# Two chained attentions on one core: weight loads in longer runs, a last block in halves, and a new hand-off table

## The chip, the cores and the metric

The kernel runs on one core of one Trainium2 chip. The metric is the device time of one execution in microseconds. The median of three runs of the kernel before is 152.31 us (150.82 to 152.47).

## What is computed

Two layers follow each other. The first is an attention with 8 heads of 64 over 768 positions, for a batch of 4, where a query sees the 8 first keys and the 96 last ones, with a bias that falls with the distance. The second is a mixture of 4 experts: each expert is a causal attention over the first layer's output, and each position adds the results of its two best experts, weighted by the gate.

```python
keep = is_global | is_local            # key < 8, or 0 <= row - key < 96
scores = np.where(keep, scale * q @ k.T - slope * dist, -1e9)
x = softmax(scores) @ v                # per head; heads side by side: B, S, 512
logits = x @ w_gate                    # the two largest of 4 -> weights w
for e in range(4):
    ye = softmax(causal(scale * (x @ wq[e]) @ (x @ wk[e]).T)) @ (x @ wv[e]) @ wo[e]
    out += (e is one of the two) * w * ye
```

## The kernel before

The rows of the batch make 24 units of 128 positions (`u`, 6 to a batch entry). Every step of a unit is a small function, a stage, and a table written as text, `ORDER` (line 791), lists the stages of all units in the order in which they are issued: two letters, the unit, and the engine of its copy (a ScalarE, g GpSimd, v VectorE) or the queue of its load (s SyncE, a ScalarE). The loop at line 765 walks through it. Each engine runs its own instructions in this order, so the table decides what is queued behind what. It comes from a planner outside the file.

The stages that matter here, in the order of a unit:

- `lk`, `lq`, `lv` (`load`, line 235): 256 KB of k, q or v as 1,024 runs of 256 bytes into one of six buffers for each of the three. `kc`, `qc` (line 256) cast to fp16; `vc`, `vx` (line 260) cast v into a ring.
- `tk`, `tq` (line 270): TensorE transposes; `tq` ends with a copy to SBUF. `gi`, `gs`: scores against the global keys. `sa`, `sb` (line 332): local scores in PSUM, with the bias added by a matmul (line 345), then an exponential on ScalarE (line 355).
- `vg`, `va`, `vb` (lines 363 and 374): the products with v. They go into a PSUM tile of which there is one buffer (`psZ`), eight heads side by side, 65 columns each, the 65th for the row sum. `vb` ends with a reciprocal (388) and a product (390) on VectorE, which leave x in fp16.
- `tx` (line 396) transposes x; `pk`, `pq` (line 405) and `pv` (line 423) project it with the weights; `ro` takes one step of the choice of experts.
- `ca`, `cb`, `cc` (line 442): causal scores and exponentials (462); `ma`: GpSimd sets the part above the diagonal to zero (474); `za`, `zb` (line 477): products with v for four experts, in the same single PSUM buffer, then reciprocal, weight and product on VectorE (494, 496, 498).
- `tz` (line 501) transposes the result, `ou` (line 514) multiplies it with wo, copies it out of PSUM (522) and stores it. Both take PSUM buffers from `psT`, which has two; scores use two of `psS`.
- `wi` and `wc` (lines 153 and 169) load and cast the weights: 0 is wk, 1 wq, 2 wv, 3 wo, 4 the gate. For 0 to 2 row d of a weight goes to partition d mod 128, so that each run of the load has 256 bytes.
- `wm` (`keep_warm`, line 241): so many matmuls of the identity, 240 columns each, into columns that nobody reads.
- `ck` (line 734) checks that all row sums lie in a safe range. At the end their count is loaded into registers (line 780), and a branch (782) goes to a general path if some did not. `bh` places a hint for this branch.

SyncE issues 56 of the 72 loads, two of the weight loads (wo and the gate) and all 24 stores; ScalarE issues 16 loads and three weight loads between its activations.

Of the kernel before, what the change touches and what calls it, by code (L numbers as in the profile page):

```python
# [18 lines left out]
P = 128  # L19
# [3 lines left out]
def kernel(  # L23
# [28 lines left out]
    NH = 3  # L52
# [30 lines left out]

    def bias_constants(_):
        V.tensor_copy(rel[:, :], rel_i[:, :])
        ge = const.tile([P, W], F32, name="ge")
        V.tensor_scalar(ge[:, :], rel[:, :], 0.0, None, op0=Alu.is_ge)
        lt = const.tile([P, W], F32, name="lt")
        V.scalar_tensor_tensor(lt[:, :], rel[:, :], float(NL), ge[:, :],
                               op0=Alu.is_lt, op1=Alu.mult)  # L90
        V.tensor_scalar(lt[:, :], lt[:, :], -1.0, -NEG, op0=Alu.add, op1=Alu.mult)
        V.tensor_scalar(rel[KB:P, :], rel[KB:P, :], slopes[1] / slopes[0], None, op0=Alu.mult)
        for p in range(NP):
            V.scalar_tensor_tensor(biasT[:, p, :], rel[:, :], -slopes[2 * p] / sc1, lt[:, :],
                                   op0=Alu.mult, op1=Alu.add)
# [57 lines left out]
    def weights_in(i, on):  # L153

        issue = queues[on]
        if i == 4:
            w32s[i] = wst.tile([P, NK, E], F32, name="wg32", tag="wg32", bufs=1)
            issue(w32s[i][:, :, :], moe_w_gate.rearrange("(ko kp) e -> kp ko e", kp=P))
            return
        w32s[i] = wst.tile([P, E, NK, Hd], F32, name="w32", tag="w32")  # L160
        if i < 3:
            issue(w32s[i][:, :, :, :],
                  (moe_wk, moe_wq, moe_wv)[i].rearrange("e (ko kp) d -> kp e ko d", kp=P))
# [35 lines left out]
    NC, current = 120, {}  # L199
# [33 lines left out]
    s16s, zs_, x16s, routing, zss, zts, tps, ppss, zs2 = ({} for _ in range(9))  # L233
# [7 lines left out]
    def keep_warm(n):  # L241
# [5 lines left out]
        for _ in range(n):  # L247
            mm(current["z"][:, 0, 4 * P - 2 * NC:4 * P].rearrange("r (a n) -> r a n", a=2),  # L248
               lhsT=ident[:, :], rhs=ident[:, 0:NC].unsqueeze(1).to_broadcast([P, 2, NC]),
               start=alone, stop=True, skip_group_check=True)  # L250
            alone = False
# [108 lines left out]
    def global_values(u):  # L360
# [3 lines left out]
        for hf in range(2):  # L364
            r = slice(hf * Dh, hf * Dh + Dh)
            mm(zs_[u][:, hf, 0:HG * VW].rearrange("r (h d) -> r h d", h=HG),  # L366
# [3 lines left out]
    def local_values(u, i):  # L370
# [4 lines left out]
        for hq in (2 * i, 2 * i + 1):  # L375
            for prev in range(2 if ri else 1):
                for c in range(2):
                    for hf in range(2):
                        r = slice(hf * KB, hf * KB + KB)
                        at = c * (2 * P - KB) + prev * P  # L380
                        mm(zs_[u][:, hf, hq * VW:(hq + 1) * VW],  # L381
# [3 lines left out]
        if i == 1:  # L385
            z4 = zs_[u][:, :, 0:HG * VW].rearrange("r a (h d) -> r a h d", h=HG)
            rinv = rinv1[:, b, ri, :].rearrange("r (a h) -> r a h", a=2)
            V.reciprocal(rinv, z4[:, :, :, Dh])
            x16s[u] = pp.tile([P, 2, HG, Dh], F16, name="x16", bufs=5)
            V.tensor_tensor(x16s[u][:, :, :, :], z4[:, :, :, 0:Dh],  # L390
                            rinv.unsqueeze(3).to_broadcast([P, 2, HG, Dh]), op=Alu.mult)

    def turn_x(u, on):

        xTs[u] = pp.tile([P, NK, P], F16, name="xT", bufs=4)
        x16 = x16s[u][:, :, :, :].rearrange("r a h d -> r (a h d)")
# [80 lines left out]
    def causal_values(u, i):  # L477
# [6 lines left out]
        z_ps = zs2[u][:, 0, 0:E * VW].rearrange("r (e d) -> r e d", e=E)  # L484
        for e in range(i * E // 2, (i + 1) * E // 2):
            for ci in range(n):
                mm(z_ps[:, e, :], lhsT=a2[:, e % 2, (e // 2) * n + ci, :],  # L487
                   rhs=held("v2buf", b * NT + ci)[:, e, :], start=(e == 0 and ci == 0), stop=True,
                   skip_group_check=True)
        if i == 0:  # L490
            return
        assert next(routing[u // NH], "end") == "end"
        rinv = rinv2[:, b, ri, :]
        V.reciprocal(rinv, z_ps[:, :, Hd])
        ce = pp.tile([P, E], F32, name="ce")
        V.tensor_mul(ce[:, :], rinv, wts[u // NH][:, ri % NH, :])
        zss[u] = pp.tile([P, E, Hd], F16, name="zs")
        V.tensor_tensor(zss[u][:, :, :], z_ps[:, :, 0:Hd],  # L498
                        ce[:, :].unsqueeze(2).to_broadcast([P, E, Hd]), op=Alu.mult)

    def turn_z(u, on):
        zts[u] = pp.tile([P, NEP, P], F16, name="zt")
        if on == "s":
            nc.sync.dma_start_transpose(zts[u][:, :, :],
                                        zss[u][:, :, :].rearrange("r e d -> r (e d)"))
            return
        zt_ps = psT.tile([P, NEP, P], F16, name="ztps", tag="t")
# [6 lines left out]
    def output(u, on):  # L514
        b, ri = divmod(u, NT)
        assert 3 in ready
        o_ps = psT.tile([P, D], F32, name="ops", tag="t")
# [5 lines left out]
        dma(out[b, ri * P:(ri + 1) * P, :], o_sb[:, :])  # L523

# [34 lines left out]
    def general_path(ctx):  # L559
# [35 lines left out]

        ident32 = gc.tile([P, P], F32, name="ident32")
# [20 lines left out]
        with tc.For_i(0, B, 1) as b:  # L617
# [43 lines left out]
            for ri in range(NT):  # L661
                l_ps = gp.tile([P, MAXB], F32, name="gs", tag="s", bufs=2)
                for ko in range(NK):
                    mm(l_ps[:, 0:E], lhsT=xT[:, ko, ri * P:(ri + 1) * P],
                       rhs=wvg16[:, ko, E * Hd:E * Hd + E],
# [6 lines left out]
            for e in range(E):  # L672
                for w, dst, nm in ((wq16, qs, "q"), (wk16, ks, "k")):
                    d = gb.tile([Hd, S], F16, name=f"g{nm}T{e}")
                    for c in range(2):
                        p_ps = gp.tile([P, MAXB], F32, name="gs", tag="s", bufs=2)
                        for ko in range(NK):
                            mm(p_ps[0:Hd, 0:S // 2], lhsT=w[:, ko, e // 2, e % 2, :],
# [6 lines left out]
                for ct in range(NT):  # L685
                    p_ps = gp.tile([P, MAXB], F32, name="gs", tag="s", bufs=2)
                    for ko in range(NK):
                        mm(p_ps[:, 0:Hd], lhsT=xT[:, ko, ct * P:(ct + 1) * P],
                           rhs=wvg16[:, ko, e * Hd:(e + 1) * Hd],
# [55 lines left out]
    def branch_hint(_):  # L745

        tc.mark_branch_hint_location("general", hint="LikelyTaken", engines=(
            mybir.EngineType.PE, mybir.EngineType.Activation, mybir.EngineType.DVE))
# [5 lines left out]
        "vs": (select_values,), "xb": (bias_constants,), "xi": (half_identities,),  # L754
# [9 lines left out]
    }  # L764
    for slot in ORDER.split():
        stage, *args = stages[slot[:2]]
        if slot[-1].isalpha():
# [7 lines left out]
    n_f = const.tile([1, 1], F32)  # L775
    V.reduce_sum(n_f[:, :], n_ps[:, :], axis=Ax.X)
    n_i = const.tile([1, 1], I32)
    V.tensor_copy(n_i[:, :], n_f[:, :])
# [13 lines left out]
xb0 lk0s kc0v lq0s az0v az1g lk1s xi0a xs0v xk0g lq1a wm14 tk0 qc0g lv0s kc1g lk2s lq2s lk3a  # L792
wm5 tq0a lq3s xc0g lv1a lv2s lq4s lk4a qc1v lq5s vc0g vx0g wm4 tk1 tq1v xm0v lk5s wm10 sa0 sb0
wm10 vs0 gi0 wi0a wm2 gs0 lk6s kc2v qc2v tk2 tq2v wm3 gs1 lq6s wm7 vg0 kc3g va0 vb0 vc1g vx1v
qc3a sa1 az2g sb1 tk3 tq3v tx0v wi1a vg1 az3g qc4a vc2g kc4g vx2v wm2 va1 wm4 sa2 sb2 vb1 qc5g
gs2 kc5a wc0g tk4 tq4v tx1v az4v lv3s vg2 va2 lv4s vb2 sa3 sb3 tk5 tq5v wm6 tx2v kc6a lq7s wi2a
qc6v wm4 sa4 sa5 tk6 vc3g tq6v pk0 sb4 sb5 wc1v pk1 wm2 gs3 wm2 pq0a vx3v pq1a gi1 vg3 vc4g
vx4g wi4s lv5s va3 vb3 lk7a ca0 ma0 pk2 pq2v tx3v ca1 vg4 va4 vb4 lq8s ca2 pk3 pq3a lk8s vc5v
vx5v cb2 vg5 wc2g lv6s kc7g lq9s pv0v pv1v lq10a lk9s qc7g qc8g kc8g ca3 cb3 tk7 lv7s tq7v pv2v
ro0 va5 sa6 tk8 tq8v tx4v vc6g vx6g lk10a lk11s vb5 sb6 gs4 lv8s ro0 pv3v pk4 qc9g pq4v ro0 ro0  # L800
lq11s lq12a ma1 vs1 lk12s lk13a sa7 tx5v kc9g pv4v kc10g ma2 vg6 va6 ro0 vb6 ca4 tk9 tq9v pk5
lk14s lq13s lv9a pq5v cb4 tx6v sb7 vc7v qc10g qc11a vx7g vc8g tk10 tq10v pv5v kc11g kc12g lq14a
qc12g cc4 vg7 va7 lq15s vb7 ro0 ro0 pk6 pq6a tk11 tq11v vx8g sa8 sb8 tx7v lk15s kc13g kc14g za0
qc13g zb0 lv10a tk12 tq12v gi2 pv6a sa9 sa10 ro1 ro1 lv11s lv12s vc9v vg8 va8 vb8 pk7 pq7a vx9g
tk13 tq13v lk16s lk17s gs5 ca5 qc14g lq16s tz0v za1 lq17s ro1 tk14 tq14v zb1 tx8a ro1 sb9 vc10g
vx10g sb10 kc15a pv7v pv8v vc11g vg9 va9 kc16a vb9 sa11 sa12 tz1v ro1 lq18s kc17v pk8 pq8a za2
ro1 tk15 zb2 sb11 sb12 qc15g tq15v tx9a vc12g vx11g vg10 va10 lk18s vx12g qc16g qc17v vb10 gs6
vs2 tk16 tq16v wi3s qc18g kc18g tk17 tq17v ma3 cb5 vg11 ma4 lk19s va11 lv13s lv14s cc5 tx10v
lv15s tk18 tq18v vb11 ca6 pv9v pv10a ro1 sa13 ro2 sa14 lq19s lq20s gi3 lq21s wc3g za3 ro2 zb3
ou0v ou1a vc13g ro2 ca7 lq22s ca8 vx13g vg12 ma5 va12 vb12 tx11v pk9 pq9v za4 ro2 lk20s kc19g  # L810
zb4 lk21s lk22s lv16s ma6 tz2a ro2 sb13 sa15 tx12v qc19v qc20g pk10 pq10a vc14g vx14g kc20g ma7
tz3v vg13 vc15g ro2 va13 vb13 lv17a cb8 gs7 ma8 ou2v tk19 tq19v lk23s lv18a za5 sb14 sb15 tz4v
zb5 tx13a pv11v sa16 ro2 sb16 vg14 va14 vb14 pk11 ro3 lv19s lv20a pq11a pv12v sa17 za6 zb6 ro3
ro3 vc16g vx15g vx16g ou3a ou4v qc21v ca9 lv21s cb9 tk20 kc21g tq20v za7 pk12 zb7 pq12a tx14v
vc17g ca10 vx17g ro3 cb10 vg15 va15 qc22g tz5v tz6v vb15 ou5a vc18g vc19g tk21 tq21v sa18 vc20v
sb17 kc22g kc23g za8 zb8 tx15a pk13 pq13v ca11 vg16 cc10 va16 pv13v lv22a pv14v cb11 ma9 vb16
gs8 ou6a pk14 pq14v ca12 vx18g vg17 va17 vb17 ca13 tz7v ro3 pk15 ro3 ro3 vx19v pq15a sb18 vs3
tx16v tx17v za9 zb9 ro4 pk16 lq23s pq16a ou7v ro4 lv23s qc23g cc11 vg18 va18 vc21g vb18 pv15a
tk22 tq22v sa19 sa20 ma10 pv16v ma11 za10 tz8a zb10 sb19 sb20 ro4 ro4 ro4 pv17v tz9v ca14 vg19
va19 vb19 ou8a ou9a vx20v sa21 sb21 ro4 ro4 tk23 tq23v ro5 za11 tx18v zb11 tz10a sa22 sb22  # L820
tx19v ma12 pv18v cb14 vg20 va20 vb20 gs9 ro5 ou10a pv19v ma13 vx21g ca15 ca16 vc22g za12 tz11v
zb12 pk17 pq17v pk18 pq18v ro5 ma14 ro5 vc23g cb15 vx22g vg21 va21 vb21 cb16 ro5 tx20v ro5 ro5
pk19 pq19a za13 zb13 pv20a ro6 sa23 sb23 tx21v vg22 va22 vb22 cc16 tz12v pk20 ro6 pq20a za14
# [47 lines left out]
```

## Time and profile before

| | before |
|---|---|
| median of 3 runs | 152.31 us (150.82 to 152.47) |
| profiled execution: its time, its span | 152.97 us, 150.8 us |
| TensorE busy | 140.3 us, 3,029 matmuls |
| VectorE, ScalarE, GpSimd busy | 111.4, 108.1, 90.2 us |
| DMA | 85,364 packets, 27.77 MB, 82,000 of them under 512 bytes |
| filler matmuls (line 248) | 75 |

The span runs from the first to the last instruction; the time of an execution holds some 2 us more around it. TensorE is PE in the views, its weight loads PEld, VectorE DVE, ScalarE ACT, GpSimd POOL, SyncE SP; a q after the name is the engine's instruction queue. A group of instructions is named by its line, its engine and the tiles that it writes and reads, and an entry of the chain by its start and its length in microseconds.

### The profile page before, as it was taken

Reading aid. Unit: us, or ns where it says so; the run is one execution under the profiler, and the core shown is the slowest. Engines: PE = TensorE matmul, PEld = TensorE weight load, DVE = VectorE, ACT = ScalarE, POOL = GpSimd, SP = SyncE. Lnnn points to the kernel's source line nnn. Section 1 sums busy time; section 2 is a strip of 40 time slices with the busy share of each in tenths; the row PEclk is TensorE's granted clock in tenths of the full one; section 3 lists DMA queues with packets and bytes.
Section 4 is the critical chain, followed back from the end, with each engine's and each line's share of the span. In section 5 each row is a group of like instructions: output and inputs, shape, how many; then the busy total and the mean of one; then the engine's idle time right before and its main releaser. Section 6 shows DMA issues by size and latency. Waiting matters only on the chain.

```text
span 150.8 us, 7217 instructions
## 1 busy us (share of the span) xinstructions
PE 140.3 (93%) x3029; PEld 110.2 (73%) x3029; DVE 111.4 (74%) x348; ACT 108.1 (72%) x176; POOL 90.2 (60%) x254
## 2 busy tenths in 40 slices
PE   5799999999999999999978999999999999999760
PEld 4567778887778888878757778888778878786520
DVE  4838676687899887878863987687787777778850
ACT  4027657778576888888638998887977978989640
POOL 7278351568878988797827899136286345463200
PEclk9999999999999999999999999999999999999999
DMA  4999998999999989899899963415221005013462
GB/s 99 280 252 286 276 261 192 254 247 238 277 282 275 245 201 249 189 256 208 231 240 288 301 166 113 116 43 142 74 77 70 4 19 195 24 51 127 155 263 97
DMA packets 85364, 27.77 MB, mean 184 GB/s; under 512 B 82000, under 2 KB 82000, under 8 KB 85328
## 3 DMA queue, kind: packets, MB, share of 16 engines
q1 hardware_dynamic: 62496, 21.51, 56.6%
q10 hardware_dynamic: 22832, 5.77, 17.1%
q8 instruction: 24, 0.39, 1.0%
q14 instruction: 12, 0.10, 0.2%
HBM read 20.98 MB, written 6.29 MB: 181 GB/s over the span
## 4 chain that ended last, share of the span: by engine, by line
PE 74%; DMA 11%; DVE 4%; POOL 3%; ACT 2%; issue 1%; SPq 1%; ACTq 0%; POOLq 0%; DVEq 0%
PE pps L414 14%; PE cps L459 7%; PE vps L428 7%; PE tp L283 7%; PE ops L519 6%; PE zps L487 6%; PE zps L381 6%; PE sps L345 5%; PE zps L248 4%; DMA kf<-in_k_dram 4%; DMA vf<-in_v_dram 4%; PE xps L402 3%; PE sps L352 3%; DMA qf<-in_q_dram 3%; PE zps L366 2%; PE ztps L509 2%
## 5 line engine op out<-in xcount | busy, mean ns | idle before, releaser
L462 ACT ACTIVATE a<-cps 128x1024 f16<-128x1024 f32 (+1 forms) x48 | 42.2, 917 | 8.3 <-PE cps L459 6.6
L355 ACT ACTIVATE abuf<-sps 128x636 f16<-128x636 f32 (+1 forms) x48 | 30.6, 686 | 12.8 <-PE sps L352 10.1
L267 POOL CAST vbuf<-vf 64x256 f16<-64x256 f32 x76 | 31.0, 408 | 8.4 <-DMA vf<-in_v_dram 5.2
L474 POOL TENSOR_SCALAR_AFFINE_SELECT a<-a 128x256 f16<-128x256 f16 x48 | 18.3, 409 | 5.1 <-ACT a L462 4.8
L285 DVE COPY kqT<-tp 128x1024 f16<-128x1024 f16 x23 | 15.7, 688 | 6.6 <-PE tp L283 6.1
L390 DVE TENSOR_TENSOR x<-zps,rinv 128x512 f16<-128x512 f32 x24 | 16.6, 691 | 0.8
L487 PE MATMUL zps<-v2buf,a 128*128 128x65 f16 x336 | 16.0, 193 | 0.6 <-DVE zs L498 0.5
L345 PE MATMUL sps<-biasT,ident 64*64 64x318 f16 (+1 forms) x192 | 14.5, 305 | 1.4 <-ACT abuf L355 1.3
L381 PE MATMUL zps<-vbuf,abuf 64*128 64x65 f16 x704 | 15.5, 189 | 0.0
L258 POOL CAST s16k<-kf 128x512 f16<-128x512 f32 x17 | 10.3, 612 | 8.7 <-DMA kf<-in_k_dram 8.3
L487 PEld LDWEIGHTS <-a 128*128 128x128 f16 x336 | 13.3, 97 | 2.1 <-DVE zs L498 0.9
L381 PEld LDWEIGHTS <-abuf 64*128 64x128 f16 x704 | 14.0, 94 | 1.1 <-issue 0.2
L414 PE MATMUL pps<-xT,wk 128*128 128x128 f16 x192 | 14.7, 219 | 0.0
L414 PE MATMUL pps<-xT,wq 128*128 128x128 f16 x192 | 14.5, 219 | 0.0
L248 PE MATMUL zps<-ident 128*128 128x240 f16 x75 | 12.8, 316 | 1.7 <-POOL ident masks.py:199 1.6
L428 PE MATMUL vps<-wvg,xT 128*128 128x260 f16 x96 | 13.9, 275 | 0.0
L459 PEld LDWEIGHTS <-kq 64*128 64x128 f16 x336 | 9.7, 94 | 5.8 <-issue 4.4
L459 PE MATMUL cps<-kq,kq 64*128 64x128 f16 x240 | 13.8, 218 | 0.0
L519 PE MATMUL ops<-wo,zt 128*128 128x512 f16 x48 | 13.5, 380 | 0.4 <-DVE zt L512 0.4
L352 PE MATMUL sps<-kqT 64*64 64x159 f16 (+2 forms) x384 | 13.8, 223 | 0.0
L258 POOL CAST s16q<-qf 128x512 f16<-128x512 f32 x15 | 9.4, 630 | 5.1 <-DMA qf<-in_q_dram 4.9
L414 PEld LDWEIGHTS <-wk 128*128 128x128 f16 x192 | 11.5, 98 | 0.8
(113 smaller groups left out, 286.4 us busy)
## 6 DMA issues: line engine op xcount, KB each, us to landing
out_dram<-osb SPq DMA_DIRECT2D x24, 256.0 KB, 2.3
qf<-in_q_dram SPq DMA_DIRECT2D x20, 256.0 KB, 5.6
kf<-in_k_dram SPq DMA_DIRECT2D x19, 256.0 KB, 5.7
vf<-in_v_dram SPq DMA_DIRECT2D x17, 256.0 KB, 5.5
vf<-in_v_dram ACTq DMA_DIRECT2D x7, 256.0 KB, 4.7
kf<-in_k_dram ACTq DMA_DIRECT2D x5, 256.0 KB, 4.9
qf<-in_q_dram ACTq DMA_DIRECT2D x4, 256.0 KB, 4.5
w<-in_moe_wk_dram ACTq DMA_DIRECT2D x1, 512.0 KB, 5.3
```

The lines of the kernel that those rows point to most:

```text
L248: mm(current["z"][:, 0, 4 * P - 2 * NC:4 * P].rearrange("r (a n) -> r a n", a=2), lhsT=ident[:, :], rhs=ident[:, 0:NC].unsqueeze(1).to_bro ...
L258: copies[on](s16s[nm, u][:, :, :], fs[nm, u][:, :, :])
L267: copies[on](o[hf * KB:(hf + 1) * KB, c, :, 0:Dh], fs["v", u][c * KB:(c + 1) * KB, hf * HG:(hf + 1) * HG, :])
L345: mm(s_ps[o, hh, 0:2 * w].rearrange("r (c n) -> r c n", c=2), lhsT=ident2[r, :], rhs=biasT[r, p, 0:w].unsqueeze(1).to_broadcast([KB, 2, w] ...
L355: S_.activation(as_[u][:, :, g, :].rearrange("r h (c n) -> r h c n", c=2)[:, :, :, 0:w], s_ps[:, :, 0:2 * w].rearrange("r h (c n) -> r h c ...
L381: mm(zs_[u][:, hf, hq * VW:(hq + 1) * VW], lhsT=as_[u - prev][r, hq % 2, hq // 2, at:at + P], rhs=held("vbuf", u - prev)[r, c, hq, :], sta ...
L414: mm(p_ps[:, i, ep, :], lhsT=w[:, ko, ep, :, :].rearrange("r a d -> r (a d)"), rhs=xT[:, ko, :], start=(i == 0 and ep == 0 and ko == 0), s ...
L428: mm(v_ps[:, :], lhsT=xT[:, ko, :], rhs=wvg16[:, ko, :], start=(ko == 0), stop=(ko == NK - 1))
L459: mm(s_ps[:, e2, i, :], lhsT=kqs[b * NT + ci][r, 0, ep, :], rhs=kqs[u][r, 1, ep, :], start=(i == 0), stop=True, skip_group_check=True)
L462: S_.activation(a2[:, :, 4 * c:4 * c + len(part), :], s_ps[:, :, 0:len(part), :], func=Exp, scale=sc2)
L487: mm(z_ps[:, e, :], lhsT=a2[:, e % 2, (e // 2) * n + ci, :], rhs=held("v2buf", b * NT + ci)[:, e, :], start=(e == 0 and ci == 0), stop=Tru ...
L519: mm(o_ps[:, :], lhsT=zts[u][:, ep, :], rhs=wo16[:, ep, :], start=(ep == 0), stop=(ep == NEP - 1))
```

## The change

1. The weights wk, wq, wv and the gate are loaded so that partition p holds the rows 4p to 4p+3: runs of 1 KB, and of 64 bytes for the gate. The columns of x are permuted to match, in the product at the end of `vb`. To make that one access pattern the heads lie 128 columns apart in the PSUM tile, 65 used; the filler writes four areas of 60 columns (`NC` 60) in place of two of 120. The general path, which no input of this size takes, loads weights of its own.
2. The last unit is worked in halves of two experts: `za` ends with its own reciprocal, weight and product, `tz` and `ty` transpose one half each, `ou` and `oy` add one half each into two output tiles of 256 columns, which VectorE and ScalarE copy and SyncE and ScalarE store. The last two units transpose, and the last three multiply, in buffers of `psS`.
3. The bias constants fall into two stages, `xb` and `xp`. The final count is reduced straight to an integer. The branch hint is placed first and names SyncE and GpSimd as well.
4. A new `ORDER`. Filler: 53 matmuls in ten stages, before 75 in fourteen. SyncE issues 58 loads and wk, wv, wo; ScalarE 14 loads, wq and the gate. Casts, copies and zero fills change engine in part.

```diff
@@ weights_in
-            issue(w32s[i][:, :, :], moe_w_gate.rearrange("(ko kp) e -> kp ko e", kp=P))
+            issue(w32s[i][:, :, :].rearrange("p k e -> p (k e)"),
+                  moe_w_gate.rearrange("(kp ko) e -> kp (ko e)", ko=NK))
...
-            issue(w32s[i][:, :, :, :],
-                  (moe_wk, moe_wq, moe_wv)[i].rearrange("e (ko kp) d -> kp e ko d", kp=P))
+            issue(w32s[i][:, :, :, :].rearrange("p e k d -> p e (k d)"),
+                  (moe_wk, moe_wq, moe_wv)[i].rearrange("e (kp ko) d -> kp e (ko d)", ko=NK))
@@ global_values, local_values
-            mm(zs_[u][:, hf, 0:HG * VW].rearrange("r (h d) -> r h d", h=HG),
+            mm(zs_[u][:, hf, :].rearrange("r (h d) -> r h d", h=HG)[:, :, 0:VW],
...
-                        mm(zs_[u][:, hf, hq * VW:(hq + 1) * VW],
+                        mm(zs_[u][:, hf, hq * P:hq * P + VW],
...
-            V.tensor_tensor(x16s[u][:, :, :, :], z4[:, :, :, 0:Dh],
-                            rinv.unsqueeze(3).to_broadcast([P, 2, HG, Dh]), op=Alu.mult)
+            x16s[u] = pp.tile([P, NK, H, Dh // NK], F16, name="x16", bufs=5)
+            V.tensor_tensor(x16s[u][:, :, :, :].rearrange("r k h d -> r h k d"),
+                            z8[:, :, 0:Dh].rearrange("r h (d k) -> r h k d", k=NK),
+                            rinv.unsqueeze(2).unsqueeze(3).to_broadcast([P, H, NK, Dh // NK]),
+                            op=Alu.mult)
@@ causal_values
+        last = u == NU - 1
+        nz = E // 2 if last else E
+        z4 = zs2[u][:, :, 0:nz * VW].rearrange("r a (e d) -> r a e d", e=nz)
...
+        z, e = (z4[:, i], slice(i * nz, i * nz + nz)) if last else (z4[:, 0], slice(0, E))
+        rinv = rinv2[:, b, ri, e]
+        V.reciprocal(rinv, z[:, :, Hd])
...
+    def end_tile(u, first, shape, dtype, name):
+        if u < first:
+            return psT.tile(shape, dtype, name=name, tag="t")
+        return psS.tile(shape, dtype, name=name, tag="s")
...
+        zt_ps = end_tile(u, NU - 2, [P, NEP, P], F16, "ztps")
...
+        o_ps = end_tile(u, NU - 3, [P, D], F32, "ops")
...
+    def last_output(ep):
...
+        for i in range(2):
+            c = slice(i * D // 2, (i + 1) * D // 2)
+            o_ps = outs["last"][i][:, :]
+            mm(o_ps, lhsT=zts[ep, "last"][:, :], rhs=wo16[:, ep, c], start=(ep == 0),
+               stop=(ep == NEP - 1), skip_group_check=True)
+        if ep == 0:
+            return
+        for i, (copy, queue) in enumerate(((V.tensor_copy, dma), (S_.copy, S_.dma_start))):
+            c = slice(i * D // 2, (i + 1) * D // 2)
+            o_sb = pp.tile([P, D // 2], F32, name=f"osb{i}", bufs=1)
+            copy(o_sb[:, :], outs["last"][i][:, :])
+            queue(out[b, ri * P:(ri + 1) * P, c], o_sb[:, :])
@@ the end
-    n_f = const.tile([1, 1], F32)
-    V.reduce_sum(n_f[:, :], n_ps[:, :], axis=Ax.X)
     n_i = const.tile([1, 1], I32)
-    V.tensor_copy(n_i[:, :], n_f[:, :])
+    with nc.allow_low_precision("whole numbers"):
+        V.reduce_sum(n_i[:, :], n_ps[:, :], axis=Ax.X)
@@ ORDER, its beginning
-xb0 lk0s kc0v lq0s az0v az1g lk1s xi0a xs0v xk0g lq1a wm14 tk0 qc0g lv0s kc1g lk2s lq2s lk3a
-wm5 tq0a lq3s xc0g lv1a lv2s lq4s lk4a qc1v lq5s vc0g vx0g wm4 tk1 tq1v xm0v lk5s wm10 sa0 sb0
-wm10 vs0 gi0 wi0a wm2 gs0 lk6s kc2v qc2v tk2 tq2v wm3 gs1 lq6s wm7 vg0 kc3g va0 vb0 vc1g vx1v
-qc3a sa1 az2g sb1 tk3 tq3v tx0v wi1a vg1 az3g qc4a vc2g kc4g vx2v wm2 va1 wm4 sa2 sb2 vb1 qc5g
-gs2 kc5a wc0g tk4 tq4v tx1v az4v lv3s vg2 va2 lv4s vb2 sa3 sb3 tk5 tq5v wm6 tx2v kc6a lq7s wi2a
-qc6v wm4 sa4 sa5 tk6 vc3g tq6v pk0 sb4 sb5 wc1v pk1 wm2 gs3 wm2 pq0a vx3v pq1a gi1 vg3 vc4g
...
+bh0 lk0s xc0g az0v lk1s lq0a az1v az2g lq1a lq2s xi0a xs0g wi4a lk2s lk3s xb0 kc0a kc1a qc0v
+qc1g wm12 tk0 xm0v lv0a wm4 tk1 lq3a tq0a wm8 tq1a az3v xk0g lq4s lv1s gi0 wm10 gs0 wm4 gs1
+lk4s xp0 qc2v wm3 sa0 kc2g kc3g tk2 sb0 vc0v vx0g qc3g qc4g tk3 lv2a tq2v wm4 vs0 lk5s wm4 tq3v
+sa1 lq5s vc1g wi0s wm2 sb1 vg0 va0 wi1a vb0 kc4g lv3s lv4s gs2 vx1g sa2 vc2g vx2v qc5g lk6s tk4
+tq4v kc5v sb2 az4g vg1 va1 vb1 sa3 sb3 tk5 tx0a tq5v lq6s wc0g wc1g vc3g vg2 va2 vb2 sa4 sa5
+wi2s tx1v tx2a lk7a wm2 gs3 pk0 lq7s lv5a lk8s kc6a sb4 vx3v lq8s pk1 pq0v lv6s vc4g vx4g pq1v
+qc6v vg3 va3 vb3 wc2g lq9s ca0 pk2 pq2a tk6 tq6v kc7v sb5 ca1 tx3v vg4 va4 vc5g qc7v ca2 tk7
...
@@ ORDER, its end
-ck0 ck1 ca23 bh0 cb23 za21 tz19v zb21 ou18v cc23 tz20v ma22 za22 zb22 tz21a ou19a ou20v ma23 za23 tz22v
-zb23 ou21a ou22a tz23v ou23a ck2
...
+cc22 ro7 ca23 tz18v ou17v za21 zb21 tz19a cb23 ou18v cc23 ck0 ck1 ma22 ma23 za22 tz20v tz21v
+zb22 ou19a ou20v ou21a za23 tz22a zb23 ou22a tz23v ty23v ou23 ck2 oy23
```

## What the change will do to the time

> **What bounds the kernel now.** I read the page first: busy shares, then the chain that ended last.
>
> ```profile
> PE 140.3 (93%) x3029; PEld 110.2 (73%) x3029; DVE 111.4 (74%) x348; ACT 108.1 (72%) x176; POOL 90.2 (60%) x254
> ...
> DMA  4999998999999989899899963415221005013462
> ...
> PE 74%; DMA 11%; DVE 4%; POOL 3%; ACT 2%; issue 1%; SPq 1%; ACTq 0%; POOLq 0%; DVEq 0%
> ...
> L248 PE MATMUL zps<-ident 128*128 128x240 f16 x75 | 12.8, 316 | 1.7 <-POOL ident masks.py:199 1.6
> L390 DVE TENSOR_TENSOR x<-zps,rinv 128x512 f16<-128x512 f32 x24 | 16.6, 691 | 0.8
> ```
>
> TensorE carries 74% of the chain, and DMA runs full until about 90 us. L248 is the filler of `keep_warm`, which computes nothing: TensorE's 93% is not all work. The windows (length, then PE, PEld, DVE, ACT, POOL, clock, DMA, GB/s) show where TensorE falls short:
>
> ```profile
> 10.00:15.00 5.00, 5.00 (x76) 3.72 (x75) 4.33 (x11) 2.57 (x6) 4.40 (x11) 1.00 1.25 282
> ...
> 70.00:80.00 10.00, 8.62 (x205) 7.03 (x203) 7.48 (x22) 5.79 (x11) 5.69 (x16) 1.00 1.01 241
> ...
> 140.00:146.00 6.00, 4.67 (x62) 2.75 (x61) 4.48 (x19) 3.16 (x6) 0.77 (x2) 1.00 0.46 175
> ```
>
> From 30 to 130 us it is full but for 1.4 us in 70-80. So time is lost at three places: filler at the front (the full 10-15 window is largely filler), a stall near 79, a ragged tail. The chain in order of time (start, length) prices them:
>
> ```profile
> 11.78 1.13 PE zps L248 x10
> ...
> 73.47 4.66 DMA qf<-in_q_dram
> ...
> 78.20 0.39 ACTq L238
> ...
> 79.29 0.71 ACT abuf L355
> 80.00 0.04 issue
> 80.04 0.33 PE sps L345 x4
> ```
>
> Ten fillers take 1.13 us, 113 ns each. At 78.20 ScalarE issues a load that had to wait; the exponential L355 is queued behind it and TensorE behind that. The waits give 2.3 us to this exponential and 1.3 us to TensorE (L345 <- L355). The end:
>
> ```profile
> 143.39 0.36 PE zps L487 x12
> 143.75 0.00 issue
> 143.75 0.60 PE ops L519 x2
> 144.36 0.02 issue
> 144.38 0.59 ACT osb L522
> 144.98 0.04 issue
> 145.02 0.29 PE ztps L509 x2
> ```
>
> The transposes of the last unit wait for an output copy that holds a PSUM buffer. Copy L522 follows at 146.32-146.91; the last DMA issue ends at 147.26, its landing takes some 2.3 us by the page's table, and SyncE's waits and closing barrier fill the rest to 150.8.
>
> [...] 241-282 GB/s in windows full of 256 B packets, 379 GB/s in 146-147, where 2 KB output rows move. [...] L390 (N=512) gives 691, as measured; no trace row strides as the new one does. [...] the longest gaps are 1.4-1.6 us and the clock stays full.
>
> **The change, part by part.**
>
> *Weights.* Three tensors of 512 KB go from 2,048 packets each to 512, the gate from 512 to 128: 4,992 fewer. At 282 GB/s the 1.57 MB take 5.6 us; at 379 they would take 4.2. Saving 0 to 1.4; with the gate (384 packets at the 256 B rate, one per 256 B/282 GB/s = 0.9 ns: 0.35) I take 1.2 us of DMA, in the supply-bound front. Casts keep count and size; wq's moves to POOL: four of about 400 ns, 1.6 us, in a 20-30 window with POOL 4.29 of 10 busy. If that cover went, queries of the projections would be 1.6 us late.
>
> *Permuted x.* The same 512 elements in L390, read at a stride of four words, written in runs of 16: 0 [...]. Head areas start every 128 words, so the writes of L366 (48) have gaps[...]. Within a run the words stay adjacent; I take 0, bound 0 to one more pass of 260 columns at 110 ns (L428's 1.00 us for x8 in the chain is 125): up to 6 us. No reason for a gain in either.
>
> *Front order.* Filler falls from 75 to 53: 22 x 113 ns = 2.5 us. That is worth its price only if work is ready. Before `pk0` both tables want 20 loads and the weights; ones for wk and wq now arrive in 1 KB runs, and the new table puts `pk0` ahead of unit 6's transposes. DMA gives 1.2 of the 2.5 outright; placing `pk0` earlier moves work into the filler's place (8 matmuls each for wk and wq, 0.9 us). I take 2.0; bounds 0.3 and 3.5. The bias products leave the first DVE block (1.03 us for x4) and come after two casts: off the path, since `sa0` now follows `gs1`. The selection's four copies (0.32 us of DVE) go to POOL, one pair of zero fills comes back; at 3-4 us of 5 busy both have room before 15 us. Hints on SyncE and GpSimd: about 50 ns before SyncE's first load.
>
> *Queues.* SyncE goes from 56 loads and 2 weights (gate, wo) to 58 and 3 (wk, wv, wo); ScalarE from 16 loads and 3 weights to 14 and wq and the gate. That is 3 issues less on ScalarE, 0.4 us each, 1.2 us in all. SyncE's longest stays, up to 3.7 us an issue, are back-pressure; behind them only loads and outputs wait. Four of ScalarE's loads come late in the old table (`lv17a`, `lv18a`, `lv20a`, `lv22a`), two of them in its window 74-79, beside the stall; the new has `lv13a` and `lv17a`. So the 79 us stall should go: 1.3 us; bounds -1.5 (another such wait) and 2. What is late next is DVE and POOL at 74-91% in 50-60 and 80-90, behind a full TensorE.
>
> *Copies that change engine.* Projection copies: 5 of qk to DVE (690 against 586 ns), 5 of v back to ScalarE (374 against 425): 5x690-5x425 = +1.3 us on DVE, three casts of k at about 0.45 more, less wq's cast (1.5), three z copies (0.9) and two v casts (0.6): near 0 of 111. ScalarE: -2.9+1.9+1.1, near 0.
>
> *Tail.* PSUM buffers of the score pool serve the last units: the transposes no longer wait for copies (0.2+0.2), nor value products for DVE directly (0.5, three outputs now lie in that wait): 0.7. After the last L487 (143.75) the copy ended at 146.91: 3.16 us. In halves: reciprocal 0.17, weight 0.16, [...] one transpose 0.25, half copy 0.25, two 256-column matmuls 0.35, the check's DVE work ahead of the copy 0.2, half copy 0.42, gaps 0.2: 2.3. Gain 0.85. One more DMA (ScalarE, 128 KB) runs beside the other; 3 small DVE instructions hide behind the second half's matmuls. Against it stands the count: SyncE reaches its waits only through the branch at about 148.7, 0.8 us before they ended at 149.5 (answer for line 782); one conversion (0.14) goes there. I cap the tail's 1.55 at 1.3; bounds 0.6 and 1.6.
>
> Sum: 2.0 + 1.3 + 1.3 - 0.05 = 4.55 us. Span 150.8 - 4.55 = 146.3; the profiled time of 152.97 (2.2 around the span) becomes 148.4. The median shown, 152.31, lies 0.66 under that execution; I carry the sum to it: 147.7.
>
> **Rivals.** (1) *Supply stays the bound.* The loads still come at one 256 KB per us, TensorE waits where it used to idle with filler, the stall near 79 moves: front 0.4, tail 1.3: 150.6. For it: full DMA slices to 90 us. Against: 1.57 MB in a quarter of the packets, ahead of everything that depends on it. (2) *Slower: the clock gate at the front.* No filler follows `pk0` in the new table, and 22 are gone. [...] Against: gaps so far are 1.5 us or less. A gapped or strided access at its upper bound (6 us, on TensorE's path) would end at about 154 too (152.3 - 4.6 + 6). (3) *The change isn't what it says:* packets stay 256 B. Source and tile are contiguous over 1 KB, so hardly; it would leave 149.
>
> **How the numbers follow.** Forecast, 145.2 to 149.8: 0.60; better than that: 0.04; rival 1 with (3), 149.8 to 152.6: 0.20; rival 2 and the access bounds, above: 0.16. About 1% can be told from no change, 150.8 to 153.8. Faster: 0.64 and half of rival 1, 0.74; same: 0.12, with the mildest of the slow cases; slower 0.14. The range, 145.2 to 152.6, leaves 0.2 outside; its low end is 3.5 + 2 + 1.6 = 7.1 below the median.
>
> **What would show it.** Packets: 85,364 - 4,608 - 384 + 128 (last unit's 1 KB rows) + 16 = 80,516. L248 x53 at 113 ns and `pk0` some 2 us before its 26.0. L390 still 691 ns; L366 pairs still 0.29. Windows at 70-80 over 9.5. The last osb copy within 2.5 us of the last value products. A TensorE clock under full at 15-30, an L390 over 1.0 us, or ScalarE held at a load for 2 us would make it wrong.

## The result: slower by 7%, and the profile after

| | before | after |
|---|---|---|
| median | 152.02 us (150.82 to 152.47, 4 runs) | 162.47 us (161.91 to 163.22, 4 runs) |
| after / before | | 1.070 [1.062, 1.078] |
| profiled span | 150.8 us | 159.0 us (time 161.91) |
| mean of the 256-byte packets, 5 to 60 us | 18.2 ns | 22.8 ns |
| first projection matmul (`pk0`) | 25.87 us | 29.65 us |

The forecast was 147.7 us, faster. Here and below medians are of all runs, ratios of undisturbed runs alone; the profiled execution of before, at 152.97 us, is longer than its median. The page of the changed kernel, the lines that answer to those of before:

```profile
PE 140.4 (88%) x3009; PEld 109.5 (69%) x3009; DVE 110.8 (70%) x341; ACT 109.3 (69%) x179; POOL 92.6 (58%) x262
...
DMA  4999999999999999999999906993103110124354
GB/s 95 223 216 218 221 282 235 256 220 188 224 212 225 222 189 237 207 199 286 219 253 217 231 6 210 237 217 108 36 6 136 66 70 4 70 87 171 147 205 137
DMA packets 80517, 27.78 MB, mean 175 GB/s; under 512 B 75488, under 2 KB 77280, under 8 KB 80480
...
PE 62%; DMA 23%; DVE 8%; POOL 2%; issue 2%; ACT 1%; SPq 0%; DVEq 0%; POOLq 0%
...
L397 DVE TENSOR_TENSOR x<-zps,rinv 128x512 f16<-128x512 f32 x24 | 16.6, 691 | 0.8
```

The packets fell as planned, and the strided product (L397) takes its old 691 ns. But DMA's share of the chain doubled, from 11% to 23%. The DMA row is as full as before for 90 us, yet the GB/s row says 216 to 223 in slices 2 to 4, where the page of before has

```profile
GB/s 99 280 252 286 276 261 192 254 247 238 277 282 275 245 201 249 189 256 208 231 240 288 301 166 113 116 43 142 74 77 70 4 19 195 24 51 127 155 263 97
```

A full queue with fewer bytes: each packet takes longer. Windows of the changed kernel (length, PE, PEld, DVE, ACT, POOL, clock, DMA, GB/s):

```profile
10.00:15.00 5.00, 5.00 (x44) 3.41 (x44) 0.67 (x2) 2.04 (x4) 3.04 (x6) 1.00 1.35 218
...
50.00:60.00 10.00, 6.94 (x159) 5.73 (x156) 6.77 (x23) 5.09 (x9) 7.39 (x19) 1.00 1.12 208
...
70.00:80.00 10.00, 8.18 (x182) 6.10 (x175) 6.85 (x21) 6.50 (x13) 7.44 (x17) 1.00 1.20 246
```

Half of the 44 matmuls of the first window are filler (22), where before there were 76, 27 of them filler. The column's clock of 1.00 counts from 13.85 us, where the record of the clock begins (before: 10.29); until then filler is slow, ten matmuls in 2.0 us where the chain of before has ten in 1.13. TensorE, full from 30 to 70 us before, now has holes there; its longest waits, for casts of k and q (L289, 6.5 us in all), hang on loads.

### The profile page after: what moved, and what is told of

It is laid out like the page before. It is cut to its first block, busy times and chain, and to the rows that moved or that the text cites. A ratio compares the mean times of both kernels' runs of the same rounds, so it can differ in the third digit from the quotient of the medians.

```text
span 159.0 us, 7178 instructions
## 1 busy us (share of the span) xinstructions
PE 140.4 (88%) x3009; PEld 109.5 (69%) x3009; DVE 110.8 (70%) x341; ACT 109.3 (69%) x179; POOL 92.6 (58%) x262
## 2 busy tenths in 40 slices
DMA packets 80517, 27.78 MB, mean 175 GB/s; under 512 B 75488, under 2 KB 77280, under 8 KB 80480
## 4 chain that ended last, share of the span: by engine, by line
PE 62%; DMA 23%; DVE 8%; POOL 2%; issue 2%; ACT 1%; SPq 0%; DVEq 0%; POOLq 0%
DMA qf<-in_q_dram 10%; PE pps L423 10%; DMA kf<-in_k_dram 8%; PE zps L498 6%; PE ops L534 6%; PE cps L468 6%; PE vps L437 5%; PE tp L289 5%; PE zps L387 5%; DMA vf<-in_v_dram 4%; PE sps L351 4%; PE xps L411 3%; PE sps L358 3%; PE zps L254 3%; PE ztps L524 2%
## 5 line engine op out<-in xcount | busy, mean ns | idle before, releaser
L273 POOL CAST vbuf<-vf 64x256 f16<-64x256 f32 x80 | 32.2, 403 | 15.6 <-DMA vf<-in_v_dram 12.3
L483 POOL TENSOR_SCALAR_AFFINE_SELECT a<-a 128x256 f16<-128x256 f16 x48 | 18.4, 412 | 8.8 <-ACT a L471 8.5
L291 DVE COPY kqT<-tp 128x1024 f16<-128x1024 f16 x22 | 15.1, 687 | 9.2 <-PE tp L289 8.9
L397 DVE TENSOR_TENSOR x<-zps,rinv 128x512 f16<-128x512 f32 x24 | 16.6, 691 | 0.8
L387 PEld LDWEIGHTS <-abuf 64*128 64x128 f16 x704 | 14.5, 95 | 0.7 <-issue 0.2
L289 PE MATMUL tp<-ident,s16k 128*128 128x128 f16 x96 | 10.0, 231 | 5.5 <-ACT s16k L264 2.5
L358 PEld LDWEIGHTS <-kqT 64*64 64x64 f16 x384 | 11.3, 108 | 3.0 <-issue 2.2
L468 PE MATMUL cps<-kq,kq 64*128 64x128 f16 x240 | 13.1, 218 | 0.0
L289 PEld LDWEIGHTS <-s16k 128*128 128x128 f16 x96 | 6.3, 101 | 8.7 <-ACT s16k L264 3.4
```

The costliest lines, as they stand in the source:

```text
L273: copies[on](o[hf * KB:(hf + 1) * KB, c, :, 0:Dh], fs["v", u][c * KB:(c + 1) * KB, hf * HG:(hf + 1) * HG, :])
L289: nc.tensor.transpose(tps[u][:, i, p, :], s16[:, p * P:(p + 1) * P], ident[:, :])
L358: mm(s_ps[o, hh, c * w:c * w + n], lhsT=kqT[b][r, 0, p, k0:k0 + KB], rhs=kqT[b][r, 1, p, k0:k0 + n], start=False, stop=True, skip_group_ch ...
L387: mm(zs_[u][:, hf, hq * P:hq * P + VW], lhsT=as_[u - prev][r, hq % 2, hq // 2, at:at + P], rhs=held("vbuf", u - prev)[r, c, hq, :], start= ...
L468: mm(s_ps[:, e2, i, :], lhsT=kqs[b * NT + ci][r, 0, ep, :], rhs=kqs[u][r, 1, ep, :], start=(i == 0), stop=True, skip_group_check=True)
```

## The experiments

Ratios are to the kernel before, timed beside each experiment, with 95% intervals. "Mean" is that of all 256-byte packets of the profiled execution.

### 1. Where the packets land

The removed constant `n_f` occupied 32 bytes of each partition in the pool that lies ahead of all other buffers. By the allocation in the compiled programs, the load buffers of k, q and v began at a multiple of 256 bytes before (78,336) and 32 bytes lower after (78,304, 224 past a multiple). Theory A: that makes each packet dearer.

`a1_after_aligned` is the changed kernel with an unused constant in `n_f`'s place:

```diff
+    const.tile([P, 8], F32, name="pad")
```

> The changed kernel with one unused constant of 32 bytes per partition put back, so that the load buffers start at multiples of 64 bytes (and of 256) again, as before; nothing else moves. Theory A (the buffers slid by 32 bytes and every 256-byte packet of a load got slower): packets of 256 bytes take 18 ns again, TensorE is full from 30 to 90 us, and the time is 146 to 150 us. Theory B (the new table or its division over the two rings starves TensorE): packets stay at 22 to 25 ns and the time at 161 to 163 us.

Measured: 154.51 us, 1.016 [1.012, 1.019]; mean 18.1 ns. About eight microseconds of the loss were the address. The rest of the loss stays: the 146 to 150 us of theory A were not reached.

`a2_before_shifted` is the kernel before with only the change that removes the constant:

```diff
-    n_f = const.tile([1, 1], F32)
-    V.reduce_sum(n_f[:, :], n_ps[:, :], axis=Ax.X)
     n_i = const.tile([1, 1], I32)
-    V.tensor_copy(n_i[:, :], n_f[:, :])
+    with nc.allow_low_precision("whole numbers"):
+        V.reduce_sum(n_i[:, :], n_ps[:, :], axis=Ax.X)
```

> The kernel before with one part of the change alone: the final count reduced straight to an integer, so that the 4-byte constant n_f is gone (it holds 32 bytes) and all buffers behind it lie 32 bytes lower. Old table, old weights. Theory A: packets of 256 bytes at 22 to 25 ns and a time of 158 to 164 us. Theory B: 18 ns and 151.5 to 152.5 us, as before less 0.14 us.

Measured: 164.51 us, 1.074 [1.054, 1.094]; mean 22.4 ns. One edit at the very end of the kernel slows its front.

`a3_before_64` is the kernel before with an unused constant of 64 bytes (load buffers 64 past a multiple of 256):

> The kernel before with an unused constant of 64 bytes, so that the load buffers start 64 bytes past a multiple of 256. If theory A holds with a grain of 64 bytes: 18 ns a packet, 152 us. If its grain is 256 bytes, the length of a run: 22 to 25 ns and 158 us or more. Theory B: 152 us.

Measured: 160.74 us, 1.051 [1.038, 1.064]; mean 21.3 ns. A multiple of 64 isn't enough.

These moved every buffer behind the constants. `b1_raw_shifted` moves the load buffers alone to 224 past a multiple, `b2_raw_128` to 128 past one; the pools behind keep their old residue:

```diff
+    gap = fast.enter_context(tc.tile_pool(name="gap", bufs=1))
+    gap.tile([P, 56], F32, name="gap")        # b2: [P, 32]
     raw = fast.enter_context(tc.tile_pool(name="raw", bufs=6))
+    rest = fast.enter_context(tc.tile_pool(name="rest", bufs=1))
+    rest.tile([P, 8], F32, name="rest")       # b2: [P, 32]
```

> The kernel before with one difference: the SBUF buffers that the k, q and v loads land in begin 32 bytes short of a multiple of 256 (224 of 256), by an unused tile ahead of them; a second unused tile puts all buffers behind them back on their old residue. Theory A (the address that the 256-byte packets land at sets their time): 160 to 165 us, packets at 22 to 25 ns, as when everything was shifted. Rival (it was the address of some other buffer, such as those of exponentials, of x or of the mask, that cost the time): 152 to 153 us and 18 ns.

> The kernel before with only the load buffers moved, to 128 past a multiple of 256. Theory A with a grain of 128 bytes: no change, 152 to 153 us and 18 ns. Theory A with a grain of 256 bytes: [...] 158 to 162 us and 21 to 25 ns, as with a shift of 64.

Measured: b1 164.17 us, 1.084 [1.079, 1.090], mean 22.8 ns; b2 163.65 us, 1.075 [1.067, 1.083], mean 22.2 ns. The rival falls, and so does the grain of 128; b2 even lies above the 158 to 162 us expected. The page of b1; the queues' rows are packets, MB and share of 16 engines' span:

```profile
DMA  4999999999999999989999999341520102311363
GB/s 110 223 218 218 222 220 187 221 208 215 209 231 221 220 219 202 224 169 253 216 226 236 222 259 245 94 130 38 134 108 31 65 4 84 121 65 66 142 251 141
...
q1 hardware_dynamic: 62496, 21.51, 62.3%
q10 hardware_dynamic: 22832, 5.77, 20.9%
```

and that of before:

```profile
q1 hardware_dynamic: 62496, 21.51, 56.6%
q10 hardware_dynamic: 22832, 5.77, 17.1%
```

The same packets and bytes took 83.2% of 161.7 us in place of 73.7% of 150.8 us: 134.5 against 111.1 us of all 16 engines, 21% more for nothing but an address.

The source rows keep their place and the destination moved: from 5 to 60 us the mean is 18.2 ns at 0, 22.7 at 64, 23.9 at 128 and 24.1 at 224 past a multiple.

The three means past a multiple differ mostly by how dense the loads were. From 10 to 15 us the packets of all five misaligned kernels (the changed one, a2, a3, b1, b2) take 25.1 to 25.9 ns and bring 218 GB/s; those of before take 18.0 ns and bring 279. In b1 from 28 to 30 us, at 210 GB/s and the same residue, they take 18.5 ns. So the price was no fixed time on each packet: off a multiple of 256 bytes dense loads stayed near 218 GB/s, some 850 packets a microsecond, and there the packets grew to 25 ns.

One trace says more. In a3 the weights happen to land at a multiple. From 18 to 21 us they alone fill ScalarE's queue, 571 packets a microsecond, while SyncE's queue brings k and q at 64 past, 541 packets, and all take about 18.4 ns. So 1,112 packets a microsecond, about half of them misaligned, went through at 18.4 ns, where 850 that are all misaligned took 25. Why a misaligned packet costs more isn't shown; that the residue sets the price under dense loads is.

### 2. The table with the buffers in place

`a4_old_table` is the changed code, aligned, with the order table of before (the four new stages inserted):

```diff
 ORDER = """
-bh0 lk0s xc0g az0v lk1s lq0a az1v az2g lq1a lq2s xi0a xs0g wi4a lk2s lk3s xb0 kc0a kc1a qc0v
+xb0 xp0 lk0s kc0v lq0s az0v az1g lk1s xi0a xs0v xk0g lq1a wm14 tk0 qc0g lv0s kc1g lk2s lq2s lk3a
...
```

> The changed kernel with the order table of before (with the two half stages of the last unit and the split bias stage put where they belong) and with the buffers at multiples of 64 bytes. Weights in 1 KB runs, permuted x, last unit in halves. Theory A: 18 ns a packet, a time near 150.5 us: the tail's 1.3 us alone, since the old filler and the old stall near 79 us remain. Theory B: 150 to 152 us as well; against the first run of this call it gives what the new table is worth.

Measured: 152.66 us, 1.001 [0.996, 1.006], 2 us over the 150.5 expected. So the new table is what costs the remaining 1.6%, and weights, halves and the rest bring nothing that shows in this form.

Is the new table short of loads in the middle? `c1_new_half_v` (new table) and `c2_old_half_v` (old table) load half of v:

```diff
-        queues[on](f[:, :, :], {"k": k, "q": q, "v": v}[nm][b, :, ri * P:(ri + 1) * P, :]
+        n = HG if nm == "v" else H
+        queues[on](f[:, 0:n, :], {"k": k, "q": q, "v": v}[nm][b, 0:n, ri * P:(ri + 1) * P, :]
...
-                           fs["v", u][c * KB:(c + 1) * KB, hf * HG:(hf + 1) * HG, :])
+                           fs["v", u][c * KB:(c + 1) * KB, 0:HG, :])
```

> The changed kernel with aligned load buffers (as a1_after_aligned, new table), loading only heads 0 to 3 of v and casting these twice: it leaves out half of v, 3.1 of 18.9 MB of loads. Theory (with loads at their old rate, the new table's stalls between 30 and 70 us are waits for loads that its faster front reached too early): the stalls at L290 and at the global values go, TensorE is full from 30 to 70 us, and the time is 149 to 151 us, no more than the old table with the same omission. Rival (the new table's own order makes TensorE wait for VectorE, ScalarE or GpSimd): the stalls stay, 153 us or more, still 1.5 to 2 us above the old table with the same omission.

> As a4_old_table (changed code, order table of before, aligned load buffers), with the same omission of half of v: the control for c1_new_half_v. Theory: the old table hardly waits for loads after 20 us, so little changes, 151.5 to 152.7 us. Rival (loads bound the old table as well): 150 us or less.

Measured: c1 152.31 us, 1.005 [1.001, 1.009]; c2 152.67 us, 1.012 [1.007, 1.017]. The old table gains nothing from fewer bytes (by its ratio it even loses 1% to a4, which I can't explain); the new one gains 1% on a1 and loses its handicap against the old, but it doesn't reach the 149 to 151 that I gave it. Bytes are part of the cause, not all.

`d2_new_less_filler` is a1 less the new table's last five fillers:

```diff
-qc2v wm3 sa0
+qc2v sa0
...
-tq2v wm4 vs0 lk5s wm4 tq3v
+tq2v vs0 lk5s tq3v
...
-wi0s wm2 sb1
+wi0s sb1
...
-lk7a wm2 gs3
+lk7a gs3
```

> The changed kernel with aligned load buffers and the new table (as a1_after_aligned), less its last five fillers (15 of 53 matmuls, 1.7 us). Theory (under the new table TensorE waits for loads between 30 and 70 us, so time won ahead of them is only waited out): within 0.4 us of a1_after_aligned, 1.01 to 1.02 of before. Rival (the middle's stalls come of the order of its own work and not of when loads land): about 1.5 us less than a1_after_aligned, 1.00 to 1.006 of before.

Measured: 153.38 us, 1.011 [1.008, 1.015]: 1.7 us of filler gave some 0.7, give or take 0.8. Its chain and its windows show one place:

```profile
13.94 0.01 ACT abuf L362
13.95 6.50 DMA vf<-in_v_dram
20.45 0.02 issue
20.47 0.04 DVE vbuf L274
20.51 0.27 issue
20.77 0.40 DVE vbuf L274
21.17 0.03 issue
21.20 0.70 DVE kqT L292
21.90 0.04 issue
21.94 0.48 PE sps L359 x8
```

```profile
21.00:22.00 1.00, 0.06 (x4) 0.06 (x7) 0.97 (x3) 0.00 (x0) 0.89 (x3) 0.94 1.25 313
22.00:23.00 1.00, 0.96 (x21) 0.64 (x20) 1.00 (x2) 0.53 (x1) 1.00 (x4) 0.50 1.11 250
```

The new table gives v of unit 2 to ScalarE (`lv2a`), behind an exponential; in both tables one of its casts is on VectorE (`vx2v`), ahead of a copy `kqT` that the scores wait for. Issued at 13.95 us, it landed at 20.45; before, SyncE issued it at 8.86 and it had landed at 15.04. TensorE stands for 2.61 us and has half its clock for the next 3.4 us. The changed kernel itself shows the same (issued 16.02, landed 22.73, a gap of 2.0 us and a clock of 0.50 from 24.1 to 27.5). Where this load lands sooner (17.73 in a1, 18.14 in e1 below) the gap isn't there, and TensorE waits later instead: the late v can't be what a1 and e1 lose by.

`e1_new_two_z` is the new table, aligned, with the change to the tail that section 4 describes:

> The changed kernel with aligned load buffers and the new table (as a1_after_aligned), with the last unit's second half of value products in a PSUM tile of its own (as b3_two_z). The wait of that half for VectorE (0.67 us in a1_after_aligned) goes; some 0.4 to 0.6 us less than a1_after_aligned, 1.010 to 1.013 of before. The front loses nothing to filler here; theory: TensorE's losses between 20 and 70 us are waits for casts of loads that VectorE, in its order, holds. Rival: the rest of the new table's loss lies in the tail: then within 0.5% of before.

Measured: 153.66 us, 1.019 [1.015, 1.023]; the 0.4 to 0.6 us expected of the tail don't show, and the rival that the loss lies there falls. Windows of e1:

```profile
40.00:50.00 10.00, 8.96 (x232) 7.47 (x233) 7.40 (x22) 6.62 (x11) 6.91 (x18) 1.00 1.04 234
50.00:60.00 10.00, 9.83 (x223) 8.20 (x216) 8.71 (x26) 8.46 (x15) 9.35 (x25) 1.00 1.03 234
60.00:70.00 10.00, 9.27 (x217) 7.44 (x215) 7.78 (x23) 6.82 (x13) 7.74 (x19) 1.00 1.10 266
```

Its first projection is at 24.15 us, 1.7 earlier than before; at 30 us it has issued 425 matmuls besides filler, before 393. At 60 us both have the same 54 units of 256 KB landed (48 of k, q and v and three weights), but it has issued 1,071 and before 1,094: the lead is gone. d2, which lost its time at 22 us and is full from 30 to 60, stands at 1,071 as well. More than that the counts don't tell: executions of the old table stand between 1,067 (b3) and 1,102 (a4) at 60 us, and the two executions compared took almost the same time, 152.77 us in e1 and 152.97 before. Where e1 loses its 1.9% they don't show.

### 3. Filler and weights need each other

`b4_less_filler` is the old table with the changed code and the tail of section 4, less the last four fillers; `c3_before_less_filler` is the kernel before, less the same four (the words of `ORDER` around each):

```diff
-tq5v wm6 tx2v
+tq5v tx2v
...
-qc6v wm4 sa4
+qc6v sa4
...
-pk1 wm2 gs3 wm2 pq0a
+pk1 gs3 pq0a
```

> As b3_two_z, less the last four fillers of the front (6, 4, 2 and 2 matmuls of the identity, 14 in all, 1.6 us at 113 ns each). If this filler stood in the way of ready work, 1.0 to 1.5 us less than b3_two_z, near 150.3 us. If loads bound the front, TensorE waits instead and the time stays within 0.3 us of b3_two_z.

> The kernel before, less the same last four fillers of the front (14 matmuls, 1.6 us). If the 1.1 us that their removal gave with the changed code depended on the weights landing sooner, this stays within 0.4 us of before, near 151.8. If it is the filler alone, it gains 0.8 to 1.3 us: near 150.6.

Measured: b4 150.76 us, 0.995 [0.993, 0.997]; c3 150.99 us, 0.995 [0.992, 0.998]. These 14 matmuls stood in the way, with or without the change: they gave 1.1 us against b3, 0.7 against before.

`c4_still_less` and `d1_before_still_less` take three more fillers out of the two:

```diff
-lq6s wm7 vg0
+lq6s vg0
...
-vx2v wm2 va1 wm4 sa2
+vx2v va1 sa2
```

> As b4_less_filler, less three more fillers (7, 2 and 4 matmuls, 13 in all, 1.5 us), which stand between 16 and 23 us. If this filler too stood in the way of ready work, about 1 us less than b4_less_filler, near 149.7 us; if TensorE then waits for the loads, the same as b4_less_filler within 0.3 us.

> The kernel before, less seven fillers of the front (27 of 75 matmuls, 3.1 us at 113 ns), as in c4_still_less but with nothing of the changed code. If the earlier weights (1 KB runs), halves and other code are worth nothing of their own, the same as c4_still_less: near 149.5 us. If the earlier weights are what lets the removed filler pay (the DMA saving of 1.2 us of the prediction), c4_still_less stays 0.8 to 1.2 us ahead: near 150.4 us.

Measured: c4 149.42 us, 0.987 [0.983, 0.991]; d1 151.59 us, 0.999 [0.995, 1.003]. Now the changed code matters. `e2_plain_weights` is c4 with the weights' loads and x as before, `e3_still_less_again` is c4, beside it:

```diff
-                  (moe_wk, moe_wq, moe_wv)[i].rearrange("e (kp ko) d -> kp e (ko d)", ko=NK))
+                  (moe_wk, moe_wq, moe_wv)[i].rearrange("e (ko kp) d -> kp e ko d", kp=P))
...
```

> As c4_still_less, with the weights and the gate loaded as before (256-byte and 16-byte runs) and x in its plain order; everything else of c4_still_less is kept. If the 1 KB runs are what put it ahead of d1_before_still_less: 1.0 to 1.5 us more than c4_still_less, 0.995 to 1.0 of before. If the halves of the last unit and the rest did it: within 0.4 us of c4_still_less.

> c4_still_less once more, unchanged, beside e2_plain_weights on the same chip, as its control: 0.983 to 0.990 of before.

Measured: e2 151.57 us, 1.001 [0.999, 1.004]; e3 149.09 us, 0.987 [0.983, 0.991]. The 1 KB runs, with the permuted x that they need, are worth 0.0139 of 151 us, 2.1 us, give or take 0.7 from the two intervals. The window from 20 to 25 us of e2, then of e3:

```profile
20.00:25.00 5.00, 3.57 (x101) 2.58 (x98) 3.22 (x9) 2.78 (x5) 1.12 (x4) 1.00 1.02 219
```

```profile
20.00:25.00 5.00, 4.75 (x122) 3.62 (x115) 4.19 (x12) 3.62 (x7) 1.97 (x5) 1.00 0.93 214
```

In e3 wk, wq and wv land at 17.8, 20.9 and 29.7 us, in e2 at 18.6, 22.0 and 31.0. But wk is there long before the first projection, which starts at 23.46 against 25.07. What TensorE waits for in e2, 1.07 us, is the cast of k of unit 6, whose transposes stand ahead of `pk0`: that load lands at 21.68 us in e3 and at 23.46 in e2. So weights that take less of the queues pay by letting the loads behind them land sooner. Part of the 2.1 us may be an address again: in both, by the same allocation, the weights land 192 past a multiple of 256, and up to 25 us e2's 256-byte packets take 0.7 us of all 16 engines above 18 ns each, e3's 0.06. 256-byte runs of weights at a multiple weren't timed.

`d3_least_filler`, c4 less two more (`wm10` ahead of `vs0`, `wm3` ahead of `gs1`):

> As c4_still_less, less two more fillers (10 and 3 matmuls, 1.5 us), which stand between 12 and 18 us. If loads bound the front by now: within 0.4 us of c4_still_less, 0.983 to 0.989 of before. If not: about 1 us less, 0.98 of before.

Measured: 150.37 us, 0.993 [0.989, 0.996], no faster than c4 and slower than either guess. Its chain runs from 18.77 to 23.66 us through the load of a q, whose cast the transposes ahead of the first projection wait for: there the loads bound the front. Why it is slower than c4 is open. c4 is the best version found, 149.42 us and, as e3, 149.09.

### 4. The tail

In a4, TensorE near the end (start, length, engine, line, idle before it):

```profile
143.29 0.53 PE L499 MATMUL zps<-v2buf,a 128*128 128x65 f16 x12 [0.96 <-DVE zs L512]
```

and VectorE ahead of it:

```profile
141.95 0.69 DVE L538 COPY osb<-ops 128x512 f32<-128x512 f32 x1 [0.38 <-ACT osb L538]
142.55 0.16 DVE L509 RECIPROCAL rinv<-zps 128x2 f32<-128x2 f32 x1
142.75 0.16 DVE L511 TENSOR_TENSOR ce<-rinv,wt 128x2 f32<-128x2 f32 x1
142.95 0.29 DVE L512 TENSOR_TENSOR zs<-zps,ce 128x128 f16<-128x128 f32 x1
```

The second half's products go into the same PSUM tile as the first half's and wait until VectorE has read that; and VectorE first finishes an output copy. `b3_two_z` gives the second half a buffer of `psT`:

```diff
+        if last and i:
+            zs2[u] = psT.tile([P, 1, nz * VW], F32, name="zps3", tag="t")
...
```

> The changed code with the order table of before and aligned load buffers (as a4_old_table), and one difference: the second half of the last unit's value products goes into a PSUM tile of its own. Theory (the halves gave nothing because the second half's products, in the same PSUM tile, waited 0.96 us for VectorE to finish the first half): that wait is gone and the kernel ends 0.8 to 1.0 us earlier, near 151.7 us. Rival (the last copy, store and closing set the end): within 0.3 us of a4_old_table's 152.66.

Measured: 152.06 us, 1.002 [1.000, 1.004]; no gain against a4 that the timing tells. The wait did go; the products end before 143.3, and the wait that is left is one for a copy:

```profile
142.83 0.44 PE L501 MATMUL zps<-v2buf,a 128*128 128x65 f16 x9
143.10 0.59 PE L537 MATMUL ops<-wo,zt 128*128 128x512 f16 x2
144.06 0.61 PE L537 MATMUL ops<-wo,zt 128*128 128x512 f16 x2 [0.37 <-DVE zt L530]
```

From the 20 products that follow the last wait for `zs` of the unit before to the end of the last output copy, ScalarE's in all three, it is 5.94 us before (140.97 to 146.91), 6.16 in a4 (139.91 to 146.07) and 5.58 in b3 (140.48 to 146.06). So in these executions, one of each, the new tail as made cost 0.22 us and with two tiles brought 0.36; b3's execution entered its tail 0.57 later than a4's.

## Why the prediction was wrong, step by step

- **The final count** is the step that failed. I valued it as "one conversion (0.14)". The conversion did go, but with it 32 bytes of a constant, and with these the place of every buffer behind. Price: 1.070 against 1.016, 8 us. Nothing that I read in the profile of before shows it; the diff did: it removed an allocation, and I asked only what it removed in instructions. Without this step the forecast is still wrong: a1 lies 1.6% above before, not 3% below, by the steps that follow.
- **Weights.** The packets came out at 80,517, forecast 80,516. The 1.2 us of DMA was low: 2.1 us where TensorE can use it, part of it perhaps an address (section 3). That it gave "1.2 of the 2.5 outright" was wrong: beside the old filler it gave nothing (a4), and less filler without it gave nothing at seven fillers (d1). Each alone leaves the other as the bound.
- **Permuted x and gapped PSUM.** Right: L397 takes 691 ns, and the pairs of L372 0.28 us for two matmuls. No row of before had such an access; the 0 was my estimate.
- **Front order, 2.0 us.** Its sign held at the front with aligned buffers (`pk0` 1.7 us sooner in e1, 2.1 in a1), and in e1 all of it was lost by 60 us. The working of this step stopped at `pk0` and took a lead there for a lead at the end.
- **Queues.** The stall at 79 us went (70 to 80 us is 10.00 in e1). I counted ScalarE's issues and looked at the late ones; the one that hurt the changed kernel and d2 is early, `lv2a`. That step named what is queued behind a held load, but not what is late when a load is itself queued behind an exponential. A run that moves this load alone wasn't made.
- **Tail, 1.3 us.** Failed: the 0.85 for halves took the second half's products to run while VectorE works on the first, but in one PSUM tile they waited 0.96 us for it. The product of a half, an estimate in the 2.3 us, took the 0.29 us given to it (a4, L512). With two tiles the whole tail brought 0.36; the 0.7 given to the score pool's buffers wasn't tried alone.
- **Hints, 50 ns.** The first load is issued 0.10 us later, behind a hint on SyncE that took 46 ns (at 0.81 us). Besides, the time of an execution less its span is 2.07 us on average in the runs of before, 2.43 in a4 and 2.69 in a1. So some 0.6 of a1's 2.4 us lies where no trace shows it. The hints are a candidate; they weren't tried alone.
- **Rivals.** Rival 1 (supply) is nearest to the aligned kernel, but its 150.6 kept the tail's 1.3, which never came. Rival 2, a halved clock after one long wait at the front, for 154.7 us, did occur in its clock: 0.50 for 3.41 us after gaps of 2.61 us (d2) and 2.0 us (the changed kernel). That one gap decides was my estimate, and so was the price; that 154.7 is a1's 154.51 is luck, for a1's clock is 1.00 in every window up to 146 us. Rival 3 fell with the packet count. None has the address in it.

The sum: 147.7, plus 4.6 of forecast gain that didn't come, plus 2.2 that the aligned kernel loses to the 152.3 it started from, plus 8.0 for the address, is 162.5. What stays open is the split of the new table's 1.6%: the late v (in d2 and the changed kernel), the later waits and the time outside the span are seen, but only bytes and filler were varied.

## What to carry to other kernels

An edit that adds or removes a tile, however small, moves what is allocated behind it: compare the addresses of DMA destinations modulo 256 bytes before any timing is read, above all where packets are 256 bytes and loads are dense (here 32 bytes cost 8 us). Filler and supply hid each other here (1.001 and 0.999 for one alone, a4 and d1, 0.987 for both, c4), so shorten them together and judge each by the pair. A lead at one point may be lost again, as e1's 1.7 us at `pk0` was by 60 us, with no more loads landed than before.

## What was not expected of the hardware

- From 5 to 60 us the 256-byte packets into SBUF took 18 ns where the destination is a multiple of 256 bytes, and 23 to 24 on average at 64, 128 or 224 past it. From 10 to 15 us they brought 218 GB/s at each of the three residues, 279 at a multiple. A kernel with 73,728 to 79,872 of them lost 5 to 8%.
- Gaps of TensorE of 2.61 us (d2) and 2.0 us (the changed kernel) were followed by 3.41 us at a clock of 0.50; gaps of 2.25 us (the changed kernel, at 50.6) and 2.26 us (b1, at 7.5) were not. So the length of one gap didn't decide here. In the records the stretches of one clock, but the last, are whole multiples of 3.41 us (10.24, 3.41 and 129.71 us in the changed kernel, 139.95 in before), so I cut time into such pieces. Between 12 us and the tail, half clock followed the four pieces in which TensorE was busy least, 0.86 (d2), 1.54 (the changed kernel), 1.70 (a3) and 1.82 us (a2), and no piece with 1.83 or more. The gap of 2.25 us fell into two pieces. Earlier pieces with as little as 1.40 us (b1) kept their clock, so this is an ordering, not a rule.
